# Sets of 4, 4, 4, 4 and 2 tiles, a third place for maxima, another order of first loads, and shifted urgencies in a planned order

## The chip, the core and the metric

The kernel runs on one core of a Trainium2 chip. The metric is the device time of one execution in microseconds (us), lower being better; the kernel before takes 776.19 us, the median of three runs (775.37 to 777.86).

## What is computed

Three layers follow one another on a batch of 4 sequences of 576 positions and 512 features.

```
scores = q k^T / 8, masked: 32 positions back (heads 0-3) or every 4th of 128 back (heads 4-7)
x   = softmax(scores) v                     # 4 x 8 heads x 576 x 64, joined to 4 x 576 x 512
h   = relu(x w_in)                          # 512 -> 1024
g   = sigmoid(conv3 over positions of h)
y   = (h * g) w_out                         # 1024 -> 512
u   = y + real(fft over features(fft over positions(y)))
un  = (u - mean(u)) / sqrt(var(u) + 1e-6)   # by row
out = u + relu(un w_ch1) w_ch2              # 512 -> 2048 -> 512
```

Rows of the output are held as 18 tiles of 128 positions by 512 features.

## The kernel before

**A planned order.** The program is first written down as a list of works (class `Plan`). A work is one instruction, or one group of matmuls that stay together (`products`), and it has the engines that may do it with a cost for each, its operands, and a `key`: the time by which it is wanted. `order()` lowers each key below those of the works that need it, and then simulates all engines with those costs; at each step the engine that is free first takes the work with the smallest key among those that are ready. The order that comes out is the order in which each engine's instructions are issued, and on the chip each engine works through its own in that order.

**Attention, stage one.** `tick(n)` does one of 56 pieces (14 for each of the 4 sequences; a piece is 4 blocks of queries of two heads). TensorE forms scores in PSUM (for sequences 0 and 1 a matmul with the mask goes first, and ScalarE copies the scores to a tile `sm`; for 2 and 3 VectorE adds the mask on the way to `sm`). GpSimd finds the maximum over partitions (`partition_all_reduce`, into a ring `mxs` of 2 tiles). VectorE subtracts it, ScalarE takes the exponential, TensorE multiplies with v (with a column of ones, for the sum). VectorE adds 1e-9 to the sums (tile `rs`) and takes the reciprocal; ScalarE scales the four blocks with it, in four instructions (`normed`, line 605, tile `xb`). TensorE transposes, ScalarE and VectorE write the result as a high and a low part (`copy`, `lo_of`) into `x`. Every product of stages two to four is made of three matmuls of such parts (`mm3`).

**The gated layer, stage two.** For each sequence and each of 8 blocks of 128 hidden features, `m1` makes two halves of 288 columns in PSUM, through one bank for the first three sequences, which ScalarE empties with a relu into `hp`; convolution, tanh and the gating follow on VectorE and ScalarE, and the result goes as high and low part to `hid_t`. `m2` uses four blocks of 128 columns of it as stationary operands, beginning at columns 0, 128, 288 and 416 (`COLS`), and adds into banks 4 to 7. The weights come as 64-bit floats in a staging tile `raw`, and VectorE turns each block into high and low part (`convert`: three bit operations, then a subtraction).

**The Fourier layer, stage three.** `dft(b)` takes a sequence's folded rows through tables (tile `tb`, loaded by GpSimd's DMA queue), adds to y and stores tiles of u. `ln` normalises rows: `bn_stats`, `bn_aggr` and 13 small VectorE operations for a group of tiles, then a ScalarE scaling, four transposes and a split for each tile. In `dft(1)` the tiles of the second set are normalised at once and stored (`to_dram`), among them tile 16, in a group of its own.

**The last layer, stage four.** The 18 tiles are worked through in sets (`SETS`: 4, 5, 5 and 4 tiles); for each set and each of 16 blocks of 128 hidden features, `n1` makes the hidden block for all tiles of the set and `n2` multiplies it, tile by tile, into one PSUM bank per tile. `n1` of a set of 4 is 12 matmuls of 512 columns. A set of 5 has 640 columns, more than a bank holds, so that `n1` is 24 matmuls of 320 columns. `n2` is three matmuls of 512 columns for each tile. `runs` gives the order of the sets and their banks; the first set begins inside stage three and is finished after the second. `lns` says in which steps of one set the next set's tiles are loaded and normalised.

Of the kernel before, what the change touches and what calls it, by code (L numbers as in the profile page):

```python
# [25 lines left out]
HS = S // 2  # L26
# [158 lines left out]

LAT = {"PE": 0.25, "DVE": 0.12, "ACT": 0.15, "POOL": 0.2, "SP": 0.0, "NO": 0.0}
# [5 lines left out]
class Plan:  # L192
# [98 lines left out]

    def order(self):
# [6 lines left out]
        for w in reversed(W):  # L299
            us = min(w.where.values()) + (2.0 if w.bytes else 0.0)  # L300
            for s in w.succ:
                w.key = min(w.key, W[s].key - us - 0.1)
# [115 lines left out]
def tile_kernel(ctx: ExitStack, tc: tile.TileContext, forms, qt_in, ktp, ktd, vtp, vtd, wm1, wm2, conv_w,  # L418
# [63 lines left out]
    hid_t = moe.tile([128, 2, 2, 640], F32R, "hid")  # L482
# [4 lines left out]
    gh_t, gl_t = ([hid_t[:, i, l, :S] for i in range(2)] for l in range(2))  # L487
# [54 lines left out]
    mxs = att.ring(2, [128, 384], F32, "mx")  # L542
    rss = att.ring(3, [128, 4], F32, "rs")
    xbs = att.ring(3, [128, 4, D], F32, "xb")
    tiny = att.tile([32, 8], F32, "tiny")

# [17 lines left out]
    def tick(n, sb, pb, at, spare_dve, less=False):  # L564
# [26 lines left out]
        with P.products(at + 5):  # L591
# [3 lines left out]
        dve("tensor_scalar", 0.15, out=rs.unsqueeze(2), in0=pv[:nq, :, 64:65], scalar1=1e-9, scalar2=None,  # L595
            op0=ALU.add)
# [9 lines left out]
        P.add({"ACT": 0.92} if less else {"DVE": 0.42}, normed, [pv[:nq, :, 0:64], rs], [xb])  # L606
# [34 lines left out]
    COLS = [0, 128, 288, 416]  # L641
    hid = {}

    def m1(b, f, h_banks, at):
# [24 lines left out]
        copy(gh, g, ("ACT", "POOL"))  # L669
        lo_of(gl, g, gh)  # L670

    def m2(b, f, at):
        gh, gl = hid[NF1 * b + f]
        w = W1.tiles[1, f]
        for i in range(4):
            c0 = COLS[i]
            with P.products(at + 2.15 * i):
                mm3(bank[4 + i], gh[:, c0:c0 + 128], gl[:, c0:c0 + 128], w[:, 0], w[:, 1], f == 0, f == NF1 - 1)
        for src, dst in ((gh, g9h), (gl, g9l)):
            sv = src.bitcast(F32).rearrange("p (t s) -> p t s", t=2)[:, :, 256:288]  # L680
# [161 lines left out]
    def dft(b, at, every):  # L842
# [94 lines left out]
        if bp:  # L937
            y9 = yload(16 + pr)
            finish(16 + pr, y9, *products(lambda l, c: t9[0][:, l, c], lambda l, c: t9[1][:, l, c], a09))
            if b == 1:  # L940
                ln([y9], [lambda: to_dram(8)], df, when[0] + 8)
# [5 lines left out]
    SETS = (range(0, 4), range(4, 9), range(9, 14), range(14, 18))  # L947
    R0 = 8
    runs = ((0, 0, R0, (4, 5, 6, 7)), (1, 0, 16, (0, 1, 4, 5, 6)), (0, R0, 16, (7, 0, 1, 4)),
            (2, 0, 16, (5, 6, 7, 0, 1)), (3, 0, 16, (4, 5, 6, 7)))  # L950
# [70 lines left out]
    dve("memset", 0.05, out=tiny)  # L1021
    P.run({"POOL": 7.0}, "partition_all_reduce", out_ap=tiny, in_ap=tiny, channels=32,
          reduce_op=bass_isa.ReduceOp.max, key=-100)
    P.key = -50
    P.key = -60
    for t in QT[:1]:
        dve("memset", 0.35, out=t[64:128, 0, :])
        dve("memset", 0.35, out=t[0:64, 1, :])
    dma(KT[0][:, 0:608], ktp[0])
# [198 lines left out]
```

## Time and profile before

| | before |
|---|---|
| median of 3 runs | 776.19 us (775.37 to 777.86) |
| the profiled execution | 778.47 us |
| its span, first to last instruction | 776.7 us |
| TensorE (PE) busy | 744.8 us (96%) |
| weight loads (PEld) busy | 663.2 us (85%) |
| VectorE (DVE) busy | 486.7 us (63%) |
| ScalarE (ACT) busy | 308.6 us (40%) |
| GpSimd (POOL) busy | 135.9 us (17%) |
| mean granted TensorE clock | 0.984 |

The span is part of the profiled execution's own time; 1.8 us lie around it. That execution was 2.3 us longer than the median of the runs. Matmuls are pipelined, so the time that a group of them takes is read from its start to the start of the next group, not from the durations. L259, L246 and L605 are lines of helpers through which many instructions pass, so that the names of the tiles tell what an instruction is.

### The profile page before, as it was taken

Reading aid. Unit: us, or ns where it says so; the run is one execution under the profiler, and the core shown is the slowest. Engines: PE = TensorE matmul, PEld = TensorE weight load, DVE = VectorE, ACT = ScalarE, POOL = GpSimd, SP = SyncE. Lnnn points to the kernel's source line nnn. Section 1 sums busy time; section 2 is a strip of 40 time slices with the busy share of each in tenths; the row PEclk is TensorE's granted clock in tenths of the full one; section 3 lists DMA queues with packets and bytes.
Section 4 is the critical chain, followed back from the end, with each engine's and each line's share of the span. In section 5 each row is a group of like instructions: output and inputs, shape, how many; then the busy total and the mean of one; then the engine's idle time right before and its main releaser. Section 6 shows DMA issues by size and latency. Waiting matters only on the chain.

```text
span 776.7 us, 11954 instructions
## 1 busy us (share of the span) xinstructions
PE 744.8 (96%) x4438; PEld 663.2 (85%) x4438; DVE 486.7 (63%) x1155; ACT 308.6 (40%) x792; POOL 135.9 (17%) x151
## 2 busy tenths in 40 slices
PE   5889989999999999989999999999999999999997
PEld 4779879998999998867788999988889999988886
DVE  5989989889888788979677667317544111121112
ACT  3877766675667655434332122112212111101110
POOL 4654424542445112201000000000000000000000
PEclk9979999999999999989999999999999999999999
DMA  9944354223412835357947333005131000030001
GB/s 239 254 152 134 107 164 139 88 72 111 152 48 90 285 120 163 107 190 250 330 162 246 136 133 135 1 1 163 42 105 32 28 1 1 1 122 1 1 0 55
DMA packets 38976, 88.58 MB, mean 114 GB/s; under 512 B 4351, under 2 KB 9859, under 8 KB 38790
## 3 DMA queue, kind: packets, MB, share of 16 engines
q1 hardware_dynamic: 38262, 84.66, 34.1%
q0 software_dynamic: 432, 2.97, 1.0%
q8 instruction: 35, 0.57, 0.3%
q10 hardware_dynamic: 224, 0.18, 0.1%
q14 instruction: 23, 0.19, 0.1%
HBM read 65.23 MB, written 22.44 MB: 113 GB/s over the span
## 4 chain that ended last, share of the span: by engine, by line
PE 53%; DVE 1%; ACT 0%; issue 0%; ACTq 0%
PE pb L259 53%; DVE y L246 0%; DVE hid L246 0%; DVE win L246 0%; DVE pm L246 0%; DVE raw L246 0%; DVE hp L246 0%; DVE pp L246 0%; ACT pq L246 0%; ACT pm L246 0%; ACTq L246 0%
## 5 line engine op out<-in xcount | busy, mean ns | idle before, releaser
L259 PE MATMUL pb<-wf,hid 128*128 128x512 f32 x1140 | 291.5, 397 | 1.2 <-DVE hid L246 1.2
L259 PEld LDWEIGHTS pb<-wf,hid 128*128 128x128 f32 x1140 | 207.6, 189 | 39.1 <-DVE hid L246 1.6
L246 DVE SCALAR_TENSOR_TENSOR hid<-pb,hid 128x320 fp32r<-128x320 f32 (+1 forms) x96 | 53.5, 557 | 186.5 <-ACT hid L246 186.4
L246 ACT ACTIVATE hid<-pb 128x320 fp32r<-128x320 f32 (+1 forms) x96 | 47.1, 491 | 256.7 <-PE pb L259 256.7
L259 PE MATMUL pb<-x,wf 128*128 128x288 f32 x768 | 116.6, 302 | 3.3 <-DVE wf L246 2.0
L259 PEld LDWEIGHTS pb<-x,wf 128*128 128x128 f32 x768 | 108.8, 191 | 7.0 <-DVE wf L246 2.2
L259 PE MATMUL pb<-unt,wf 128*128 128x320 f32 x672 | 103.6, 309 | 0.0
L259 PEld LDWEIGHTS pb<-unt,wf 128*128 128x128 f32 x672 | 100.8, 188 | 2.3
L246 POOL PARTITION_ALL_REDUCE mx<-sm x56 | 82.9, 1486 | 80.6 <-DVE sm L246 39.5
L259 PE MATMUL pb<-wf,wf 128*128 128x512 f32 x336 | 85.1, 400 | 3.6 <-DVE hid L246 3.6
L259 PEld LDWEIGHTS pb<-wf,wf 128*128 128x128 f32 x336 | 64.0, 193 | 17.5 <-DVE hid L246 4.3
L605 ACT ACTIVATE xb<-pb,rs 72x64 f32<-72x64 f32 (+1 forms) x224 | 51.2, 309 | 13.2 <-DVE rs L246 12.9
L246 DVE SCALAR_TENSOR_TENSOR cv<-hp,convw,cv 128x576 f32<-128x576 f32 x64 | 55.4, 866 | 1.3 <-ACT cv L246 0.7
L259 PEld LDWEIGHTS pb<-VT,sm 104*72 104x72 f32 (+1 forms) x448 | 41.0, 157 | 8.6 <-ACT sm L246 6.8
L259 PE MATMUL pb<-VT,sm 104*72 104x65 f32 (+1 forms) x448 | 42.8, 240 | 5.6 <-ACT sm L246 5.6
L259 PE MATMUL pb<-QT,KT 128*104 128x144 f32 (+1 forms) x224 | 44.3, 323 | 1.6 <-ACT sm L246 1.1
L259 PEld LDWEIGHTS pb<-QT,KT 128*104 128x104 f32 (+1 forms) x224 | 36.1, 191 | 7.5 <-issue 4.9
L246 ACT ACTIVATE hp<-pb 128x288 f32<-128x288 f32 x64 | 26.6, 416 | 29.9 <-PE pb L259 28.5
L246 DVE TENSOR_TENSOR wf<-raw,wf 128x512 fp32r<-128x512 f32 x44 | 31.7, 722 | 6.9 <-ACT wf L246 6.6
L246 DVE SCALAR_TENSOR_TENSOR raw<-raw,win 128x512 uint32<-128x512 uint32 x48 | 34.9, 727 | 0.9
L246 DVE SCALAR_TENSOR_TENSOR win<-raw,win 128x512 int32<-128x512 int32 x48 | 34.7, 723 | 1.0
L246 POOL CAST g<-hid 128x64 fp32r<-128x64 f32 x43 | 22.4, 528 | 73.4 <-ACT hid L246 37.1
(143 smaller groups left out, 842.6 us busy)
## 6 DMA issues: line engine op xcount, KB each, us to landing
raw<-in_wm_dram SPq DMA_DIRECT2D x48, 512.0 KB, 4.5
y<-yd SPq DMA_DIRECT2D x18, 256.0 KB, 4.2
ud<-y SPq DMA_DIRECT2D x18, 256.0 KB, 3.5
QT<-in_qt_dram SPq DMA_DIRECT2D x31, 144.0 KB, 3.4
fd<-fs SPq DMA_DIRECT2D x8, 514.0 KB, 3.9
fl<-fd SPq DMA_DIRECT2D x8, 514.0 KB, 6.3
yd<-y SPq DMA_DIRECT2D x16, 256.0 KB, 2.2
uu<-ud SPq DMA_DIRECT2D x16, 256.0 KB, 3.1
```

Source lines behind the costliest of these rows:

```text
L246: getattr(self.engines[eng], name)(**a)
L259: getattr(self.engines["PE"], name)(*[v.real() for v in a], **kw)
L605: nc.scalar.mul(out=x[:, i], in_=p[:, i], mul=r[:, i:i + 1])
```

## The change

It has seven parts. (1) `SETS` becomes 4, 4, 4, 4 and 2 tiles, with banks for each run, and `lns` follows. Tile 16 moves from the second set to the third, and so it is no longer normalised in `dft(1)`, but in stage four, with the other tiles of the third set. (2) `hid_t` grows from 640 to 768 columns, and stage two lays its two halves of 288 at columns 0 and 384, so that `m2` takes blocks beginning at 0, 128, 384 and 512. (3) The addition of 1e-9 to the sums goes from VectorE to ScalarE. (4) The scaling of `xb` goes to VectorE, as one instruction, for every second piece of the first 14; it stays on ScalarE otherwise. (5) `mxs` has three tiles. (6) The first loads are issued in another order: the bf16 identity and the first 384 columns of the mask by ScalarE's queue, k and q of the first unit (a unit is two heads of one sequence), then more of the mask, k and q of the second unit, v of the first, the other identity, k and q of the third, v of the second, and only then the first weight block `raw`; the memsets of `QT` get earlier keys. (7) After keys are lowered, 31 seeds each pick a stretch of keys (4 to 50 us long) and shift every key in it at random by up to 1, 2, 4 or 8 us; then keys are lowered again. The scratch for GpSimd's DMA descriptors goes from 2048 to 512 bytes.

```diff
--- before.py
+++ after.py
...
     __slots__ = ("where", "fn", "deps", "key", "bytes", "after", "start", "eng", "left", "ready", "succ", "id")
 
+
+NUDGES = (9, 12, 27, 33, 49, 53, 82, 92, 98, 130, 181, 284, 297, 353, 473,
+          503, 521, 594, 836, 1456, 1870, 2106, 2119, 2189, 2250, 2504, 2667, 2792, 3014, 3080,
+          3211,)
+
 LAT = {"PE": 0.25, "DVE": 0.12, "ACT": 0.15, "POOL": 0.2, "SP": 0.0, "NO": 0.0}
 
...
         return self.add({queue: 1.0 if queue == "POOL" else 0.42 if v.form.shape[0] == 128 else 0.58}, fn, ins, outs, key, nb)
 
+    def urgency(self):
+        W = self.works
+        for w in reversed(W):
+            us = min(w.where.values()) + (2.0 if w.bytes else 0.0)
+            for s in w.succ:
+                w.key = min(w.key, W[s].key - us - 0.1)
+
     def order(self):
         W = self.works
         for w in W:
...
         for w in W:
             for d in w.deps:
                 W[d].succ.append(w.id)
-        for w in reversed(W):
-            us = min(w.where.values()) + (2.0 if w.bytes else 0.0)
-            for s in w.succ:
-                w.key = min(w.key, W[s].key - us - 0.1)
+        self.urgency()
+        for seed in NUDGES:
+            rng = random.Random(seed)
+            a = rng.uniform(0, 560)
+            z = a + rng.uniform(4, 50)
+            amp = rng.choice((1, 2, 4, 8))
+            for w in W:
+                if a < w.key < z:
+                    w.key += rng.uniform(-amp, amp)
+        self.urgency()
         free = dict.fromkeys(("PE", "DVE", "ACT", "POOL", "SP", "NO"), 0.0)
         can = {e: {} for e in free}
         bus, drift = 0.0, 0.0
...
     win = stg.tile([128, 512], I32, "win")
     moe = pool_of("moe", reuse_waits="tile")
     x_odd = moe.tile([128, 4, 2, S], F32R, "x")
-    hid_t = moe.tile([128, 2, 2, 640], F32R, "hid")
+    hid_t = moe.tile([128, 2, 2, 768], F32R, "hid")
     cv_t = moe.tile([128, S], F32, "cv")
     g_t = moe.tile([128, S], F32, "g")
     hpad = [moe.tile([128, S + 2], F32, "hp") for _ in range(2)]
     moe.fill(-moe.size)
-    gh_t, gl_t = ([hid_t[:, i, l, :S] for i in range(2)] for l in range(2))
+
+    gh_t, gl_t = ([hid_t[:, i, l].rearrange("p (t s) -> p t s", t=2)[:, :, :HS] for i in range(2)] for l in range(2))
 
     low = pool_of("low", reuse_waits="tile")
     g9h, g9l = (low.tile([128, NF1, 128], F32R, "g9") for _ in range(2))
...
     QT = [att.tile([128, 2, S], F32, "QT") for _ in range(NS)]
     VT = [att.tile([128, 8, 2, 65], F32, "VT") for _ in range(NS)]
     sms = att.ring(5, [128, 384], F32, "sm")
-    mxs = att.ring(2, [128, 384], F32, "mx")
+    mxs = att.ring(3, [128, 384], F32, "mx")
     rss = att.ring(3, [128, 4], F32, "rs")
     xbs = att.ring(3, [128, 4, D], F32, "xb")
     tiny = att.tile([32, 8], F32, "tiny")
+    eps = att.tile([128, 1], F32, "eps")
 
     def kq_load(u):
         b, hp = divmod(u, 4)
...
     xT = {b: x_even if b % 2 == 0 else x_odd for b in range(B)}
     subs = [(u, t) for u in range(16) for t in range(3 if u % 4 < 2 else 4)]
 
-    def tick(n, sb, pb, at, spare_dve, less=False):
+    def tick(n, sb, pb, at, spare_dve):
 
         u, t = subs[n]
         b, hp = divmod(u, 4)
...
             for s in range(4):
                 mm(pv[:nq, s, :], sm[:, s * nq:(s + 1) * nq], vt[:nk, 2 * t + s // 2, s % 2, :], True, True)
         rs, xb = rss()[:nq], xbs()[:nq]
-        dve("tensor_scalar", 0.15, out=rs.unsqueeze(2), in0=pv[:nq, :, 64:65], scalar1=1e-9, scalar2=None,
-            op0=ALU.add)
+        P.run({"ACT": 0.21}, "activation", out=rs.unsqueeze(2), in_=pv[:nq, :, 64:65], func=AF.Identity,
+              bias=eps[:nq], scale=1.0)
         dve("reciprocal", 0.17, out=rs, in_=rs)
 
         def normed(eng):
...
             else:
                 for i in range(4):
                     nc.scalar.mul(out=x[:, i], in_=p[:, i], mul=r[:, i:i + 1])
-        P.add({"ACT": 0.92} if less else {"DVE": 0.42}, normed, [pv[:nq, :, 0:64], rs], [xb])
+        P.add({"DVE": 0.42} if n < 14 and n % 2 else {"ACT": 0.92}, normed, [pv[:nq, :, 0:64], rs], [xb])
         bt = pb[:, 260:260 + 2 * nq]
         with P.products(at + 8):
             for i in range(2):
...
         dve("tensor_tensor", 0.1, out=convw, in0=a, in1=r, op=ALU.add)
 
-    COLS = [0, 128, 288, 416]
+    COLS = [(0, 0), (0, 128), (1, 0), (1, 128)]
     hid = {}
 
     def m1(b, f, h_banks, at):
...
         dve("scalar_tensor_tensor", 0.48, out=g[:, 289:576], in0=cv[:, 575:288:-1], scalar=1.0,
             in1=hp[:, 576:289:-1], op0=ALU.add, op1=ALU.mult)
         gh, gl = hid[s] = gh_t[s % 2], gl_t[s % 2]
-        copy(gh, g, ("ACT", "POOL"))
-        lo_of(gl, g, gh)
+        gs = g.rearrange("p (t s) -> p t s", t=2)
+        copy(gh, gs, ("ACT", "POOL"))
+        lo_of(gl, gs, gh)
 
     def m2(b, f, at):
         gh, gl = hid[NF1 * b + f]
         w = W1.tiles[1, f]
         for i in range(4):
-            c0 = COLS[i]
+            t, c0 = COLS[i]
             with P.products(at + 2.15 * i):
-                mm3(bank[4 + i], gh[:, c0:c0 + 128], gl[:, c0:c0 + 128], w[:, 0], w[:, 1], f == 0, f == NF1 - 1)
+                mm3(bank[4 + i], gh[:, t, c0:c0 + 128], gl[:, t, c0:c0 + 128], w[:, 0], w[:, 1], f == 0, f == NF1 - 1)
         for src, dst in ((gh, g9h), (gl, g9l)):
-            sv = src.bitcast(F32).rearrange("p (t s) -> p t s", t=2)[:, :, 256:288]
+            sv = src.bitcast(F32)[:, :, 256:288]
             dv = dst[:, f, :].rearrange("p (t s) -> p t s", t=2)[:, :, 32 * (b % 2):32 * (b % 2) + 32]
             P.run({"ACT": 0.235, "POOL": 0.45}, "copy", out=dv, in_=sv)
 
...
         if bp:
             y9 = yload(16 + pr)
             finish(16 + pr, y9, *products(lambda l, c: t9[0][:, l, c], lambda l, c: t9[1][:, l, c], a09))
-            if b == 1:
-                ln([y9], [lambda: to_dram(8)], df, when[0] + 8)
         pair(0)
 
 
-    SETS = (range(0, 4), range(4, 9), range(9, 14), range(14, 18))
+    SETS = (range(0, 4), range(4, 8), range(8, 12), range(12, 16), range(16, 18))
     R0 = 8
-    runs = ((0, 0, R0, (4, 5, 6, 7)), (1, 0, 16, (0, 1, 4, 5, 6)), (0, R0, 16, (7, 0, 1, 4)),
-            (2, 0, 16, (5, 6, 7, 0, 1)), (3, 0, 16, (4, 5, 6, 7)))
+    runs = ((0, 0, R0, (4, 5, 6, 7)), (1, 0, 16, (0, 1, 4, 5)), (0, R0, 16, (6, 7, 0, 1)),
+            (2, 0, 16, (4, 5, 6, 7)), (3, 0, 16, (0, 1, 4, 5)), (4, 0, 16, (6, 7)))
     hidden, rings, sets = {}, {}, []
 
     def un_load(p):
...
 
     dve("memset", 0.05, out=tiny)
+    P.add({"DVE": 0.05}, lambda _: nc.vector.memset(eps.real(), 1e-9), [], [eps], -95)
     P.run({"POOL": 7.0}, "partition_all_reduce", out_ap=tiny, in_ap=tiny, channels=32,
           reduce_op=bass_isa.ReduceOp.max, key=-100)
-    P.key = -50
-    P.key = -60
-    for t in QT[:1]:
+
+    for i, t in enumerate(QT):
+        P.key = -80 + i
         dve("memset", 0.35, out=t[64:128, 0, :])
         dve("memset", 0.35, out=t[0:64, 1, :])
-    dma(KT[0][:, 0:608], ktp[0])
+    loads = [-90.0]
+
+    def first(out, in_, queue="SP"):
+        loads[0] += 1
+        dma(out, in_, key=loads[0], queue=queue)
+
+    first(ident16, ident16_in, "ACT")
+    first(maskt[:, :384], mask[:, :384], "ACT")
+    first(KT[0][:, 0:608], ktp[0])
     for h, queue in ((0, "SP"), (1, "ACT")):
-        dma(QT[0][64 * h:64 * h + 64, h, :], qt_in[0, 64 * h:64 * h + 64], queue=queue)
-    dma(ident16, ident16_in, queue="ACT")
-    dma(maskt[:, :768], mask[:, :768])
-    P.key = -50
-    for t in QT[1:]:
-        dve("memset", 0.35, out=t[64:128, 0, :])
-        dve("memset", 0.35, out=t[0:64, 1, :])
+        first(QT[0][64 * h:64 * h + 64, h, :], qt_in[0, 64 * h:64 * h + 64], queue)
+    first(maskt[:, 384:768], mask[:, 384:768])
+    P.key = loads[0] + 1
+    kq_load(1)
+    P.key += 1
+    v_load(0)
+    P.key += 1
+    dma(ident, ident_in)
+    P.key += 1
+    kq_load(2)
+    P.key += 1
+    v_load(1)
+    P.key += 1
     dma(raws[0], wm1[0, :, 0])
-    v_load(0)
-    dma(ident, ident_in)
-    P.key = -40
-    kq_load(1)
-    v_load(1)
-    P.key = -30
-    kq_load(2)
+    P.key += 1
     dma(maskt[:, 768:], mask[:, 768:])
     v_load(2)
+    P.key += 1
     dma(raws[1], wm1[1, :, 0])
     P.key = 1e9
     for t in hpad:
...
         _, i, f = W1.todo[k]
         W1.convert(place[i, f], raws[k % 2], k > 1)
 
-    EARLY, LESS = 16, 56
+    EARLY = 16
     LEAD = 8.0
 
     def ticks(b):
...
             else:
                 sb, pb = bank[0], of("v2", [1, 3])
             at = 1.6 * n if b == 0 else T0 + PER * (b - 1) - LEAD + m * (PER - 3.0) / 14
-            tick(n, sb, pb, at, b < 2, n < LESS)
+            tick(n, sb, pb, at, b < 2)
 
     def mlp1(b, f0, f1, h_banks):
         step = PER / NF1
...
             step = 1.38 * len(SETS[runs[r][0]])
             begin[r, f] = at, step
             at += step
-    lns = ({(2, 9 + i): (2, (i,)) for i in range(5)})
+    lns = {(2, 9 + i): (2, (i,)) for i in range(4)}
     lns.update({(3, 3 + i): (3, (i,)) for i in range(4)})
+    lns.update({(4, 5 + i): (4, (i,)) for i in range(2)})
     for k, (r, f) in enumerate(seq):
         if (r, f) == (1, 0):
             later = pool_of("set", "left", (low,), reuse_waits="tile")
-            sets.append(later.tile([128, 2, 4, 640], F32R, "unt"))
+            sets.append(later.tile([128, 2, 4, 512], F32R, "unt"))
             un_load(1)
         if (r, f) == (1, 2):
             wpb = pool_of("wpb", "right", (D_["pool"], keep), reuse_waits="tile")
...
 
     sketch = _bacc.Bacc("TRN2", target_bir_lowering=False, num_devices=1)
     forms = tile.TileContext(sketch).__enter__().alloc_tile_pool(name="forms", bufs=1)
-    nc = _bacc.Bacc("TRN2", target_bir_lowering=False, num_devices=1, dynamic_dma_scratch_size=2048)
+    nc = _bacc.Bacc("TRN2", target_bir_lowering=False, num_devices=1, dynamic_dma_scratch_size=512)
     arrays, args = {}, []
     for name, a in _layout(**inputs).items():
         arrays[f"in_{name}_dram"] = a
```

## Rows read from the trace of the kernel before

**Rows 1.** Stretches (us): each engine's busy time, instructions, granted clock, DMA share, GB/s.
```profile
0.00:47.40 47.40, 30.93 (x230) 27.44 (x231) 36.23 (x94) 30.36 (x104) 25.37 (x24) 0.90 0.93 243
90.00:118.00 28.00, 24.09 (x162) 21.67 (x162) 25.02 (x51) 17.34 (x46) 7.37 (x7) 0.94 0.38 121
118.00:300.00 182.00, 182.00 (x1270) 167.57 (x1269) 160.63 (x370) 119.93 (x325) 68.23 (x75) 1.00 0.39 128
...
334.00:346.00 12.00, 8.39 (x28) 6.33 (x28) 8.93 (x27) 3.06 (x7) 1.41 (x2) 0.72 0.44 158
346.00:385.00 39.00, 36.52 (x204) 30.68 (x202) 31.64 (x83) 16.93 (x38) 2.39 (x5) 1.00 0.85 284
385.00:770.00 385.00, 385.00 (x2023) 338.35 (x2024) 150.86 (x366) 73.59 (x145) 2.34 (x4) 1.00 0.21 69
```

**Rows 2.** Waits of the whole span: engine and tile, waited for; us, times, longest.
```profile
ACT hp L246 <- PE pb L259: 28.5, 37, 2.7
...
DVE rs L246 <- PE pb L259: 8.8, 13, 2.8
```

**Rows 3.** TensorE's timeline: start, us, operation, count; steps and groups of matmuls.
```profile
283.47 4.34 PE L259 MATMUL pb<-wf,hid 128*128 128x512 f32 x18
287.64 3.35 PE L259 MATMUL pb<-x,wf 128*128 128x288 f32 x24
...
401.27 1.61 PE L259 MATMUL pb<-tb,t 128*128 128x258 f32 x12
...
402.72 0.28 PE L259 MATMUL pb<-tb,a 128*128 128x258 f32 x1
...
418.87 3.68 PE L259 MATMUL pb<-unt,wf 128*128 128x320 f32 x24
...
425.81 3.68 PE L259 MATMUL pb<-unt,wf 128*128 128x320 f32 x24
...
707.20 2.88 PE L259 MATMUL pb<-x,hid 128*128 128x512 f32 x12
...
712.63 2.88 PE L259 MATMUL pb<-x,hid 128*128 128x512 f32 x12
```

**Rows 4.** Instructions by line and shape, stage four's hidden block: busy us, mean ns.
```profile
L246 DVE SCALAR_TENSOR_TENSOR hid<-pb,hid 128x320 fp32r<-128x320 f32 x64 | 31.4, 491 | 109.2 <-ACT hid L246 109.2
...
L246 ACT ACTIVATE hid<-pb 128x320 fp32r<-128x320 f32 x64 | 28.0, 438 | 145.6 <-PE pb L259 145.6
```

**Rows 5.** Timeline of VectorE and TensorE about tile 16's normalisation.
```profile
335.78 0.69 DVE L246 BATCH_NORM_STATS2 st<-y 128x6 f32<-128x512 f32 x1
...
338.91 0.16 DVE L246 SCALAR_TENSOR_TENSOR sq<-mv,sq 128x1 f32<-128x1 f32 x1
...
340.10 5.43 PE L259 MATMUL pb<-wf,wf 128*128 128x512 f32 x12 [3.61 <-DVE hid L246]
```

**Rows 6.** Timeline of the head: first matmul, first weight block, first m1.
```profile
7.41 0.48 PE L259 MATMUL pb<-maskt,ident 128*128 128x384 bf16 x1 [7.41 <-DMA maskt<-in_mask_dram]
...
9.36 0.43 DVE L246 TENSOR_SCALAR win<-raw 128x512 int32<-128x512 int32 x1 [3.13 <-DMA raw<-in_wm_dram]
...
47.44 3.33 PE L259 MATMUL pb<-x,wf 128*128 128x288 f32 x12
```

**Rows 7.** Tile rs (ns min/median/max), then instructions by line and shape (mean ns).
```profile
L605 ACT ACTIVATE xb<-pb,rs x224: 290/309/354, 15.4 to 250.4; 72x64 f32<-72x64 f32 x64, 96x64 f32<-96x64 f32 x48
L246 DVE TENSOR_SCALAR rs<-pb x56: 144/151/163, 15.0 to 249.3; 72x4 f32<-72x4 f32 x32, 96x4 f32<-96x4 f32 x24
...
L246 ACT CAST a<-a 1x32 fp32r<-1x32 f32 x8 | 1.5, 215 | 0.4 <-DVE a L246 0.3
```

**Rows 8.** DMA issues (us to landing), then timeline: the tables' issue and first use.
```profile
tb<-in_tab_dram POOLq DMA_DIRECT2D x1, 1161.0 KB, 14.6
...
250.28 1.76 POOL L288 DMA_DIRECT2D tb<-in_tab_dram  x3
...
266.57 0.96 PE L259 MATMUL pb<-tb,fl 128*1 128x290 f32 x6
```

More of the change, by code (lines that the diff above doesn't have):

```diff
@@ L1 @@
+import random
 from contextlib import ExitStack, contextmanager
```

## The prediction

> **What bounds the kernel now.** I read the stretches first [rows 1]. From 385 to 770 us TensorE is busy for the whole time at the full clock, and so it is from 118 to 300: there whatever shortens TensorE's own work shortens the kernel, and relief of other engines does nothing. The rest is lost elsewhere. From 0 to 47.4 TensorE is idle for 16.5 us, and a granted clock of 0.90 means that it ran at the lower of its two levels (1.2 instead of 2.4 GHz) for 9.5 us, half of which is lost work. From 90 to 118 it idles 3.9 us, with 1.7 more lost to a clock of 0.94 (3.4 us at the lower level). From 334 to 346 it idles 3.6 us, and a clock of 0.72, which is 6.7 us at the lower level, loses 3.4 more. From 346 to 385 it idles 2.5 us. VectorE is busy for 25.0 of 28 us in the second of these places and 31.6 of 39 in the last, so it is what TensorE waits for. Then I read the waits [rows 2] and the timelines [rows 3, 5, 6] for the prices.
>
> **Sets of 4, 4, 4, 4, 2.** A step of a set of 5 takes 425.81 - 418.87 = 6.94 us for 39 matmuls with 15,360 columns, a step of a set of 4 takes 712.63 - 707.20 = 5.43 us for 24 matmuls with 12,288 columns [rows 3]. The two give 16.9 ns for each matmul and 0.409 ns for each column: 6.94 - 1.25 x 5.43 = 0.15 us is left for 39 - 1.25 x 24 = 9 matmuls. The columns of stage four stay the same in sum. The matmuls of n1 fall from 32 x 24 + 32 x 12 = 1152 to 80 x 12 = 960, and 192 x 16.9 ns = 3.2 us. A step of the new set of two is then 18 x 16.9 ns + 6144 x 0.409 ns = 2.82 us, a shape that the trace does not have. Its nearest row is a group of 12 matmuls of 258 columns, 402.72 - 401.27 = 1.45 us [rows 3], against the 1.46 us that the two figures give for 12 of 256, so I keep the 3.2. The ends: a matmul of 256 columns costs at least its columns (105 ns) and at most one of 320 columns (148 ns), against 121.6; over 192 matmuls that is 3.2 us better or 5.1 worse, so the part is worth -1.9 to 6.4. What must stay hidden in the short step is the hidden block: ScalarE and VectorE take 0.44 + 0.49 us at 320 columns [rows 4], less at 256, while n1 of the next block covers 1.45. Half a microsecond is left for the handovers; each 0.1 us beyond it would cost 16 x 0.1 = 1.6 us.
>
> The Trainium skill (page "TensorE: Matmul & The Clock Gate", section "Back-to-back issue gap") gives the spacing of warm matmuls as columns / 2.4 GHz plus 2.5 ns. By that rule 192 matmuls fewer would save 0.5 us instead of 3.2. The steps above show a fixed part of 16.9 ns; the measurement decides.
>
> **Tile 16 out of stage three.** Its normalisation holds VectorE from 335.78 to 339.07 us, 3.3 us in fifteen small operations [rows 5]. Behind it on VectorE, which works in order, stands the low part of a hidden block, and TensorE waits 3.61 us for that. Then 12 matmuls of 512 columns last 5.43 us [rows 5], where 12 such last 2.88 at the full clock [rows 3]. Idle time and clock together cost this stretch 3.6 + 3.4 = 7.0 us. With the normalisation gone the block is ready 3.3 us earlier. So the part is worth at most 7.0, and nothing if other work takes the place. What is late next is the conversion of weight blocks, also on VectorE, busy 31.6 of the 39 us that follow. I take 5.5. In stage four the same operations are hidden: VectorE is busy 151 of 385 us there [rows 1]. The tile's four transposes cost TensorE the same in either place.
>
> **Halves at 0 and 384.** A group of 18 matmuls of m2 takes 287.64 - 283.47 = 4.17 us [rows 3], while 18 matmuls of 512 columns by the figures above would take 4.07. Half of them take their weights from columns 288 and 416. If the beginning column is the cause, these cost 11 ns more each, and the kernel has 4 x 8 x 2 x 3 = 192 of them: 2.1 us. If it is not, nothing. One group does not separate the two; I take 1.5. The copies into the gapped halves move the same elements, and I cost them at nothing: TensorE is the bound from 118 to 300.
>
> **Attention's ends.** The addition leaves VectorE 56 times, 56 x 0.151 = 8.5 us [rows 7], and comes to ScalarE 56 times. The trace has no such instruction; the nearest is a ScalarE cast of 1 x 32 at 0.215 us [rows 7], so about 12 us. For seven pieces of the first 14 the four scalings (4 x 0.309 us [rows 7]) become one VectorE operation on 256 columns, which the trace does not show either; 0.49 us for 320 columns [rows 4] bounds it above. So within the first 14 pieces ScalarE loses 8.7 - 3.0 = 5.7 us of work, and VectorE gains at most 3.4 - 2.1 = 1.3. In the head the two have 30.4 and 36.2 us of work in 47.4 [rows 1], and a piece goes through both by turns, so m1, which begins at 47.44 [rows 6], can come earlier by 0 to 5.7 us. I take 2.5, a little under half, since nothing but the chain of pieces holds m1 there and its other half is VectorE's. After the head the addition stands in ScalarE's line 42 more times. I cost it at nothing as long as ScalarE is early: it waited 28.5 us for TensorE before its relus [rows 2]. The price without that cover is in the rivals. The third place for maxima is worth nothing by itself: GpSimd is busy 25.4 of 47.4 us.
>
> **First loads.** The first matmul starts at 7.41 us, when the mask has landed [rows 6]. Half of the mask now goes first. The scores need k and q too, so I take 1.0 us (0 to 2). Against it, the first weight block, whose conversion VectorE begins at 9.36 us after 3.13 idle [rows 6], moves on SP's queue behind k and q of two units and v of two, and it is wanted in stage two, where VectorE is nearly full until 118. It costs 0 to 3.1, at most that idle time again. I take 0.5.
>
> **Shifted keys and the scratch.** The shifts reorder everything up to some 560 us of planned time. Their price has no row. They can clear at most what is idle or slow from 90 to 118 and idle from 346 to 385, 5.6 + 2.5 = 8.1 us, or add a stall like that at 334, 7.0 us. Nothing in the trace says which, so I take 0. The smaller scratch matters to the three loads of the tables: issued from 250.28, landed 14.6 us later at most, first used at 266.57 [rows 8]. Some 2 us are spare. I take 0.
>
> **The sum.** 3.2 + 5.5 + 1.5 + 2.5 + 1.0 - 0.5 = 13.2 us. The profiled execution took 778.47 us (span 776.7 and 1.8 around it), which gives 765.3. It was 2.3 us longer than the median of the runs, so the forecast for the median is 776.2 - 13.2 = 763 us.
>
> **Rivals.**
>
> A. The stall moves on. Another chain of VectorE's work, the weight conversions, stands where the normalisation stood, and what the head gains is waited for again between 90 and 118. For it: VectorE's share in both places. Against it: the 3.3 us leave VectorE for good. What is left is TensorE's own work, 3.2 + 1.5 = 4.7: 771.5 us.
>
> B. The new order also clears the 8 us of the other two places: 755 us. For it: VectorE loses 8.5 us of additions spread over the first 250 us. Against it: its work before 118 hardly shrinks.
>
> C. Matmuls cost by their columns alone, and the sets are worth nothing. Against it: the 0.15 us of a step [rows 3]. Time: 763 + 3.2 = 766. This is what the page's small fixed part would nearly make of it.
>
> D. The other side: ScalarE's line. From 47.4 to 250 us the addition waits, in order, for its product with v, and behind it stand the relus that empty the one bank of m1. VectorE waited 8.8 us at the additions in all, 0.16 for each of 56 [rows 2]. If each of the 42 later pieces holds TensorE for that and for the 0.22 us of the operation, 0.38 x 42 = 16 us are lost: 776.2 - 13.2 + 16 = 779. It decides from 13.2 / 42 = 0.31 us for each piece. Against it: ScalarE is busy 120 of 182 us from 118 to 300 and waits for TensorE, not the reverse.
>
> **How the numbers follow.** I give the forecast 0.49, A 0.20, B 0.18, C 0.07, D 0.06. The forecast's own range is 759 to 768 (the stall worth 2.5 to 7, the head 1 to 5). The range of 8 in 10 reaches below nearly to B's time, since B may come in part, and above past A's: 753 to 773. Only D and the worst of A lie above it. Within 0.3% is 773.9 to 778.5, about what a measurement of this kernel can tell from no change. Faster: the forecast, B, C and most of A, 0.88. Same: the rest of A, where the parts cancel, 0.06. Slower: D, 0.06.
>
> **What would show it.** Steps of sets of 4 at 5.43 us throughout and of the last set at 2.8. A chain of waits made of TensorE alone from about 370 us on. No gap of 3.6 us before the hidden blocks near 330, and a clock of 1.00 there. Groups of 18 matmuls of m2 at 4.07 us. m1 beginning near 44 us, and the first matmul near 6.4. Wrong it would be if TensorE's idle time from 90 to 385 us stayed near the 10 us of [rows 1] in new places, if steps of the last set were over 3.0 us, or if TensorE waited for relus of ScalarE.

## The result and the profile after

The changed kernel takes 757.65 us (median of 4 runs, 757.01 to 761.7) against 776.46 for the kernel before: a ratio of 0.9773, interval 0.9753 to 0.9792, or 18.8 us less. The forecast was 763 and the range 753 to 773. The profiled execution took 757.01 us, with a span of 755.2. TensorE is busy for 736.6 us of it (744.8 before) and idle for 18.6 (31.9 before).

The stretches of the changed kernel, in the columns of [rows 1]:

```profile
0.00:47.40 47.40, 37.78 (x283) 34.55 (x284) 36.94 (x93) 31.49 (x108) 30.47 (x27) 0.93 0.86 233
47.40:90.00 42.60, 41.21 (x305) 37.22 (x304) 41.14 (x77) 33.30 (x101) 21.55 (x21) 1.00 0.47 144
90.00:118.00 28.00, 26.56 (x189) 24.09 (x188) 26.69 (x55) 21.08 (x59) 9.93 (x10) 1.00 0.48 157
118.00:300.00 182.00, 181.76 (x1266) 166.85 (x1265) 160.11 (x348) 119.96 (x334) 73.94 (x88) 1.00 0.38 123
300.00:334.00 34.00, 34.00 (x198) 29.96 (x197) 30.70 (x85) 17.19 (x40) 3.23 (x7) 1.00 0.66 229
334.00:346.00 12.00, 10.16 (x59) 7.98 (x59) 11.70 (x29) 6.30 (x13) 2.90 (x4) 1.00 0.57 209
346.00:385.00 39.00, 39.00 (x236) 34.14 (x235) 31.09 (x70) 14.38 (x38) 1.08 (x3) 1.00 0.73 246
385.00:748.00 363.00, 363.00 (x1709) 304.00 (x1708) 138.15 (x333) 65.75 (x113) 1.63 (x2) 1.00 0.20 64
```

After 47.4 us the granted clock is 1.00 everywhere, where 90 to 118 had 0.94 and 334 to 346 had 0.72. A second execution of the same kernel (760.49 us, the last run below) shows the same clock there, but 22.6 us of idle time, so that a difference of some us in idle time between two single executions proves little. Idle time is left in the head (9.6 us, 16.5 before), a little up to 118, and 1.8 us near 340. VectorE is busy 11.70 of 12 us there, so it is still what TensorE waits for, but only briefly. The end of the chain of waits (start, us, engine and line):

```profile
343.70 0.46 DVE a L253
344.16 0.04 issue
344.20 406.98 PE pb L266 x1967
```

TensorE runs without a gap from 344.20 us to the end of its work (from 384.95 in the kernel before). What the kernel gained beyond shorter steps was therefore gained before 344.

TensorE's timeline, as in [rows 3] and [rows 6]: first matmul, first m1, groups of m2, the stretch of the old stall, steps of a set of 4 and of the set of 2.

```profile
5.12 0.48 PE L266 MATMUL pb<-maskt,ident 128*128 128x384 bf16 x1 [5.12 <-DMA maskt<-in_mask_dram]
...
41.32 2.66 PE L266 MATMUL pb<-x,wf 128*128 128x288 f32 x12
...
329.07 4.24 PE L266 MATMUL pb<-wf,hid 128*128 128x512 f32 x18
333.15 2.88 PE L266 MATMUL pb<-wf,wf 128*128 128x512 f32 x12
335.87 1.04 PE L266 MATMUL pb<-ident,y 128*128 128x128 f32 x8
336.66 2.99 PE L266 MATMUL pb<-wf,wf 128*128 128x512 f32 x12
340.85 0.96 PE L266 MATMUL pb<-tb,fl 128*1 128x290 f32 x6 [1.20 <-DVE ns L253]
...
404.45 2.88 PE L266 MATMUL pb<-unt,wf 128*128 128x512 f32 x12
407.17 2.88 PE L266 MATMUL pb<-wf,hid 128*128 128x512 f32 x12
409.89 2.43 PE L266 MATMUL pb<-unt,wf 128*128 128x512 f32 x10
...
712.99 1.60 PE L266 MATMUL pb<-unt,wf 128*128 128x256 f32 x12
714.42 1.55 PE L266 MATMUL pb<-wf,hid 128*128 128x512 f32 x6
715.80 1.60 PE L266 MATMUL pb<-unt,x 128*128 128x256 f32 x12
```

A step of 4 tiles takes 409.89 - 404.45 = 5.44 us, a step of 2 takes 715.80 - 712.99 = 2.81 (forecast 2.82). The 18 matmuls of m2 take 333.15 - 329.07 = 4.08 us (4.17 before, forecast 4.07). The normalisation of tile 16 and its 3.61 us of idle time are gone.

The operations that the trace of before did not have, by line and shape (busy us, mean ns, idle before):

```profile
L253 ACT ACTIVATE rs<-pb,eps 72x4 f32<-72x4 f32 x32 | 8.2, 256 | 5.6 <-PE pb L266 4.9
...
L253 DVE SCALAR_TENSOR_TENSOR hid<-pb,hid 128x256 fp32r<-128x256 f32 x16 | 6.8, 425 | 36.7 <-ACT hid L253 36.7
...
L253 ACT ACTIVATE rs<-pb,eps 96x4 f32<-96x4 f32 x24 | 6.1, 262 | 5.1 <-PE pb L266 4.8
L253 ACT ACTIVATE hid<-pb 128x256 fp32r<-128x256 f32 x16 | 6.1, 383 | 41.5 <-PE pb L266 39.0 <-DVE hp L253 2.4
...
L624 DVE TENSOR_TENSOR xb<-pb,rs 96x256 f32<-96x256 f32 x3 | 1.3, 421 | 0.2
```

ScalarE's additions take 14.3 us in all (estimate: 12) and the scaling on VectorE 0.42 us. In the short step the hidden block takes 0.38 + 0.43 us and stays hidden: no matmul there waits.

### The profile page after: what moved, and what is told of

It is laid out like the page before. It is cut to its first block, busy times and chain, and to the rows that moved or that the text cites. A ratio compares the mean times of both kernels' runs of the same rounds, so it can differ in the third digit from the quotient of the medians.

```text
span 755.2 us, 11432 instructions
## 1 busy us (share of the span) xinstructions
PE 736.6 (98%) x4246; PEld 641.1 (85%) x4246; DVE 478.3 (63%) x1087; ACT 309.8 (41%) x800; POOL 144.7 (19%) x159
## 4 chain that ended last, share of the span: by engine, by line
PE 54%; DVE 1%; issue 0%
PE pb L266 54%; DVE fo L253 0%; DVE ns L253 0%; DVE fs L253 0%; DVE hp L253 0%; DVE o L253 0%; DVE f L253 0%; DVE a L253 0%
## 5 line engine op out<-in xcount | busy, mean ns | idle before, releaser
L253 DVE SCALAR_TENSOR_TENSOR hid<-pb,hid 128x512 fp32r<-128x512 f32 (+1 forms) x80 | 51.0, 637 | 183.3 <-ACT hid L253 183.2
L253 ACT ACTIVATE hid<-pb 128x512 fp32r<-128x512 f32 (+1 forms) x80 | 44.5, 556 | 248.2 <-PE pb L266 231.8
L266 PEld LDWEIGHTS pb<-x,wf 128*128 128x128 f32 x768 | 106.9, 189 | 3.0 <-ACT hp L253 0.7
L266 PE MATMUL pb<-unt,wf 128*128 128x512 f32 (+1 forms) x504 | 103.5, 354 | 0.0
L253 POOL PARTITION_ALL_REDUCE mx<-sm x56 | 88.3, 1591 | 62.5 <-ACT sm L253 26.8
L266 PEld LDWEIGHTS pb<-unt,wf 128*128 128x128 f32 x504 | 85.0, 189 | 14.2
L266 PE MATMUL pb<-wf,wf 128*128 128x512 f32 x336 | 82.0, 391 | 0.0
L627 ACT ACTIVATE xb<-pb,rs 72x64 f32<-72x64 f32 (+1 forms) x196 | 44.4, 306 | 4.8 <-DVE rs L253 4.7
L253 DVE TENSOR_TENSOR sm<-sm,mx 104x288 f32<-104x288 f32 (+1 forms) x56 | 32.1, 574 | 8.5 <-POOL mx L253 8.2
L253 POOL CAST g<-hid 128x64 fp32r<-128x64 f32 x48 | 25.1, 532 | 53.4 <-ACT hid L253 28.9
```

The costliest lines, as they stand in the source:

```text
L253: getattr(self.engines[eng], name)(**a)
L266: getattr(self.engines["PE"], name)(*[v.real() for v in a], **kw)
L627: nc.scalar.mul(out=x[:, i], in_=p[:, i], mul=r[:, i:i + 1])
```

## Experiments

Each kernel was timed beside the kernel before on the same chip (775.5 to 775.6 us). A difference in us is (ratio - 1) x 775.5. The texts speak of the **planned end**: the time at which, by the plan's own costs, the last work ends when `order()` simulates the engines. It is a figure of the program, not a measurement.

### Which part gave what

**The shifts taken out** of the changed kernel.

```diff
-NUDGES = (9, 12, 27, 33, 49, ...
+NUDGES = ()
```

> The changed kernel with the list of seeds empty, so that no key is shifted; all else as in the change. Theory P (the parts add up, and the shifts clear only what is left of the idle places before 385 us): 2 to 6 us above the changed kernel's 757.7, so 760 to 764, with TensorE's idle time up by as much between 0 and 400 us and stage four unchanged. Theory S (the gain beyond the sets and the halves is made by the shifts): 10 us or more above it, 768 or later, with a stall of VectorE's making near 335 us again.

767.38 us, ratio 0.9901 (0.988 to 0.9922). All parts but the shifts give 7.7 us together, and the shifts 9.7, between the two theories' ranges; the stall near 335 us that theory S expected does not come back. TensorE's waits in this kernel from 90 to 120 and from 300 to 385, out of its timeline, and the end of its chain of waits:

```profile
93.55 0.70 PE L264 MATMUL pb<-VT,sm 104*72 104x65 f32 x8 [0.71 <-DVE x L251]
...
95.92 1.58 PE L264 MATMUL pb<-x,wf 128*128 128x288 f32 x10 [0.70 <-DVE wf L251]
...
106.21 1.72 PE L264 MATMUL pb<-x,wf 128*128 128x288 f32 x10 [2.34 <-DVE wf L251]
...
302.97 1.36 PE L264 MATMUL pb<-ident,y 128*128 128x128 f32 x8 [1.84 <-ACT y L251]
...
346.44 0.66 PE L264 MATMUL pb<-ident,y 128*128 128x128 f32 x4 [1.39 <-ACT y L251]
...
353.70 1.07 PE L264 MATMUL pb<-tb,fl 128*128 128x290 f32 x6 [0.65 <-DVE a L251]
...
353.70 406.91 PE pb L264 x1967
```

The stall of tile 16 is gone here too. What is left is above all a weight block converted too late at 106 (`wf`) and two waits for `y`. In the changed kernel neither stands; the short wait for `a` does (0.64 us at 344.20). In this pair of profiles TensorE's idle time falls from 24.6 to 18.6 us, and its busy time from 740.1 to 736.6 for the same 4246 matmuls; in this trace 90 to 118 has a clock of 0.94. In the second execution of the changed kernel the idle time is 22.6 us and the busy time 736.1, so the shorter busy time is seen in both and the idle time is not as sure.

**Sets and tile 16 alone**, put into the kernel before.

```diff
-            if b == 1:
-                ln([y9], [lambda: to_dram(8)], df, when[0] + 8)
...
-    SETS = (range(0, 4), range(4, 9), range(9, 14), range(14, 18))
+    SETS = (range(0, 4), range(4, 8), range(8, 12), range(12, 16), range(16, 18))
```

> The kernel before with the sets of 4, 4, 4, 4 and 2 tiles alone, and with them tile 16's normalisation moved from stage three to stage four; no shifts. By the steps of the prediction 3.2 us from stage four and up to 7 from the stall near 335 us: 766 to 770 beside 775.6 to 776.5 for the kernel before. Rival: only the 3.2 us of stage four come, and a stall appears elsewhere between 300 and 385 us: 772 to 773. Theory Q (the time follows the end that order() itself works out while it plans): that end is 761.7 us for this list and 768.7 for the kernel before, so 7 us less.

766.71 us, ratio 0.988 (0.9846 to 0.9914): 9.3 us faster. With 3.2 for the steps, 6 are left for tile 16 (an inference: the two were not separated). TensorE waits 2.4 us from 300 to 385 in this kernel, against 7.1 in the kernel before.

**The normalisation of tile 16 put back** into the changed kernel, as work whose result nothing reads; the tile is still normalised in stage four. Once with the seeds and once without any.

```diff
+            if b == 1:
+                ln([y9], [lambda: to_dram(8)], df, when[0] + 8)
```

> The changed kernel with the normalisation of tile 16 left in stage three as well (its result is stored and not used; stage four normalises the tile again as in the change). VectorE has 3.3 us more to do near 335 us. Theory P: the time rises by 3 to 7 us, 761 to 765, with TensorE waiting for VectorE between 320 and 350 us. Rival: the planned order with its shifts finds room for it, and the rise is under 1 us.

> The changed kernel without shifts and with tile 16's normalisation left in stage three as well (its result is stored and not used). Beside the one without shifts (767.4) it has 3.3 us more for VectorE near 335 us and no other draw of the shifts, which the earlier run with both had. If the normalisation costs what stood at 336 us before: 3 to 7 us more, 770 to 774. If the 21 us of the earlier run were its doing: 780 or more. Theory Q: the plan's own end rises from 761.5 to 763.3, so 2 us more.

With the seeds 779.2 us, ratio 1.0062 (1.0041 to 1.0083): 21.5 us over the changed kernel, which no theory had. Without, 770.61, ratio 0.9941 (0.9921 to 0.996): 3.1 us over the kernel without shifts. In each stretch of keys that holds one of the added works, every later random draw falls on another work, so the first of these kernels has shifts of other works; it says nothing of the normalisation and much of the seeds. The second shows the mechanism. Its VectorE and TensorE timelines:

```profile
331.80 0.69 DVE L251 BATCH_NORM_STATS2 st<-y 128x6 f32<-128x512 f32 x1
...
334.93 0.16 DVE L251 SCALAR_TENSOR_TENSOR sq<-mv,sq 128x1 f32<-128x1 f32 x1
...
335.37 0.68 DVE L251 SCALAR_TENSOR_TENSOR hid<-pb,hid 128x512 fp32r<-128x512 f32 x1
```

```profile
336.11 4.61 PE L264 MATMUL pb<-wf,wf 128*128 128x512 f32 x12 [3.58 <-DVE hid L251]
340.56 0.60 PE L264 MATMUL pb<-ident,y 128*128 128x128 f32 x4
```

The fifteen small operations take the same 3.3 us, the low part of the hidden block stands behind them, TensorE waits 3.58 us (3.61 in [rows 5]), and the 12 matmuls after it take 4.45 us instead of 2.7, at a clock of 0.86 from 334 to 346. These lose 5 us; in their place the kernel without shifts waits 3.2 us for `y`, and the net is 3.1.

**Halves at 288.** Only the addresses change; the order of the instructions stays.

```diff
-    gh_t, gl_t = ([hid_t[:, i, l].rearrange("p (t s) -> p t s", t=2)[:, :, :HS] ...
+    gh_t, gl_t = ([hid_t[:, i, l, :S].rearrange("p (t s) -> p t s", t=2) ...
```

> The changed kernel with the halves of the hidden block at columns 0 and 288 again; the order of all instructions is the same as in the changed kernel, only addresses differ. If the beginning column is what costs: m2 groups of 18 take 4.17 us instead of 4.08, and the whole 1.9 us more than the changed kernel, about 759.5. If it is not: m2 groups unchanged and a time within 0.5 us of the changed kernel.

757.94 us, ratio 0.9777 (0.9763 to 0.9792), which the changed kernel's 757.65 can't be told from. Its trace is finer. The same 18 matmuls, and its first m1 and the end of its chain:

```profile
41.63 2.83 PE L266 MATMUL pb<-x,wf 128*128 128x288 f32 x12
...
330.20 4.29 PE L266 MATMUL pb<-wf,hid 128*128 128x512 f32 x18
334.33 2.89 PE L266 MATMUL pb<-wf,wf 128*128 128x512 f32 x12
...
345.30 406.98 PE pb L266 x1967
```

They take 4.13 us against 4.08, and 9 of the 18 have moved, so that each costs some 5.6 ns more; a group of 21 takes 4.84 against 4.78 us, one of 12 takes 2.87 against 2.83. So in these groups the beginning column does cost; 192 x 5.6 ns would be 1.1 us in the kernel. That estimate is too high. TensorE's unbroken run begins 1.1 us later, at 345.30 instead of 344.20, but 0.3 of it is there at the first m1 and 0.7 at 115 us. Matched matmul by matmul (the order is the same), this trace falls 0.37 us behind that of the changed kernel from 118 to 344 us, 0.40 of it at the 312 matmuls `wf,hid`, where the second execution of the changed kernel falls 0.04 behind the first. Nearly half of these 312 have moved, so the mean cost is under 3 ns each, and some 0.5 us in the kernel (an estimate from 0.40 us).

**Attention's ends alone**, in the kernel before.

```diff
-        dve("tensor_scalar", 0.15, out=rs.unsqueeze(2), in0=pv[:nq, :, 64:65], scalar1=1e-9, ...
+        P.run({"ACT": 0.21}, "activation", out=rs.unsqueeze(2), in_=pv[:nq, :, 64:65], ...
...
-        P.add({"ACT": 0.92} if less else {"DVE": 0.42}, normed, ...
+        P.add({"DVE": 0.42} if n < 14 and n % 2 else {"ACT": 0.92}, normed, ...
```

> The kernel before with attention's ends alone: the addition of 1e-9 on ScalarE, and every second scaling of the first 14 on VectorE. By the prediction m1 starts 2.5 us earlier (0 to 5.7) and the time falls by as much, to 771 to 775. Rival (the head's gain is waited for again between 90 and 118 us, where VectorE is full): m1 earlier, the time unchanged at 775 to 777. Rival D (ScalarE's line holds up the relus): 779 or more. Theory Q: the plan's own end falls from 768.7 to 765.8, so 3 us less.

774.19 us, ratio 0.9982 (0.996 to 1.0004): 1.4 us faster, which can't be told from nothing. Its first m1 begins at 46.59 instead of 47.44.

**The order of first loads alone**, in the kernel before: the lines of the change from `for i, t in enumerate(QT)` to the second `raw`.

```diff
-    dma(KT[0][:, 0:608], ktp[0])
...
+    first(ident16, ident16_in, "ACT")
+    first(maskt[:, :384], mask[:, :384], "ACT")
+    first(KT[0][:, 0:608], ktp[0])
```

> The kernel before with the new order of the first loads alone. By the prediction the first matmul comes 1 to 2 us earlier and the first weight block's conversion later, with 0.5 us left of it: 774 to 776. Rival: the late weight block costs its 3 us between 90 and 118, 777 to 779. Theory Q: the plan's own end rises from 768.7 to 770.3, so 1.6 us more.

779.26 us, ratio 1.0048 (1.0028 to 1.0067): 3.7 us slower. Its trace has a first m1 at 43.80, 3.6 us earlier, and then this (stretches):

```profile
0.00:47.40 47.40, 34.91 (x257) 31.15 (x258) 36.72 (x97) 31.01 (x111) 29.24 (x27) 0.89 0.87 232
47.40:90.00 42.60, 38.75 (x286) 35.80 (x286) 36.84 (x81) 29.71 (x89) 25.37 (x21) 0.97 0.41 127
```

The kernel before, in the second of these stretches:

```profile
47.40:90.00 42.60, 42.17 (x312) 39.74 (x311) 39.48 (x84) 31.29 (x95) 21.12 (x21) 0.95 0.40 129
```

What the head gained, 4.0 us of TensorE's busy time, the next stretch gave back all but 0.6 of: 38.75 us busy against 42.17. The late weight block is not what this trace shows as the price: from 40 to 120 us TensorE waits 2.8 us for weight blocks, and 2.9 in the kernel before. The profiled execution (776.54) was the fastest of ten, and its unbroken run begins earlier than that of the kernel before (383.08 against 384.95), so where the 3.7 of the median lie it does not show.

### Shifts, or these seeds?

**Other seeds**, 31 in a row, not picked.

```diff
-NUDGES = (9, 12, 27, 33, 49, ...
+NUDGES = (100001, 100002, ..., 100031)
```

> The changed kernel with 31 other seeds (100001 to 100031), which nobody picked. Theory P: about what the kernel without shifts takes, give or take 4 us, 757 to 767, since a shift of a key matters little. Theory S, that the seeds were picked for their effect: later than the kernel without shifts, 766 or more, as random shifts of 31 stretches make stalls as often as they remove them.

766.59 us, ratio 0.9881 (0.9852 to 0.9911), like no seeds at all (767.38). These unpicked shifts are worth nothing that can be told from noise.

**The change's seeds in the kernel before**, by `urgency()` and the loop over `NUDGES` alone.

> The kernel before with the 31 seeds as the only change. Its planned end goes from 768.7 to 777.5 us. Theory Q (the seeds fit the one list of works for which they were picked, and elsewhere they are noise): slower than before by 1 to 9 us, 777 to 785. Rival (shifted keys help whatever the list, by some 5 to 10 us): 766 to 771.

777.7 us, ratio 1.0026 (1.0009 to 1.0043): 2.0 us slower. The seeds that help the changed kernel's list of works do not help this one.

**Another list, with and without seeds of its own.** The changed kernel with the first loads in the order of before: without seeds, and with 37 seeds picked by the planned end.

```diff
-    first(ident16, ident16_in, "ACT")
-    first(maskt[:, :384], mask[:, :384], "ACT")
...
+    dma(KT[0][:, 0:608], ktp[0])
...
+    dma(raws[0], wm1[0, :, 0])
```

> The changed kernel without any seeds and with the first loads in the order of the kernel before. Its planned end is 761.8 us, against 761.5 for the changed kernel without seeds, which took 767.4. Theory Q (the time follows the planned end): 767 to 768. Rival F (the new order of loads costs 3.7 us by itself, as it did when put alone into the kernel before, since the first weight block comes late): 763 to 764.

> The changed kernel, but the first loads in the order of the kernel before, and 37 other seeds, picked one after the other because each brought the planned end of the last work forward: it is 751.4 us instead of 754.6 with the change's own loads and seeds. Theory Q (the time follows the planned end, plus 3 to 9 us that the costs of the plan miss): 754 to 758 us, at or below the changed kernel's 757.7. Theory F (what the plan does not see at the head, the wait for the first weight block, is what the old order of loads also avoids on the chip): below 755 us. Rival R (the change's seeds were picked on the chip and fit it; seeds picked by the plan alone lose part of the 9.7 us): 759 to 764 us.

> The changed kernel as it is, beside the others on the same chip: 757 to 758 us.

Without seeds 769.65 us, ratio 0.9919 (0.9897 to 0.9942). With its own 37, 759.02, ratio 0.978 (0.9761 to 0.9799). The changed kernel beside them: 758.74, ratio 0.9779 (0.9759 to 0.9799). So a search over seeds gives this list 10.8 us too, and the two kernels end level; the 3 us that its planned end was ahead did not come. Nor did the loss that rival R expected of seeds picked by the plan alone. The old order of loads, without seeds, is 1.4 us slower than the new one (0.9919 against 0.9901, the intervals overlapping): the 3.7 us that the new order costs in the kernel before are not found among the other parts, and the 763 to 764 of rival F did not come.

Planned end and time stand side by side in this table, each as a difference to the kernel before, in us:

| kernel | planned end | time |
|---|---|---|
| the change | -14.0 | -17.1 to -17.6 |
| without shifts | -7.2 | -7.7 |
| other seeds | -4.8 | -9.2 |
| tile 16 also, with the seeds | +4.7 | +4.8 |
| tile 16 also, no seeds | -5.3 | -4.6 |
| sets and tile 16 alone | -6.9 | -9.3 |
| attention's ends alone | -2.9 | -1.4 |
| first loads alone | +1.6 | +3.7 |
| the seeds alone | +8.9 | +2.0 |
| old loads, no seeds | -6.9 | -6.3 |
| old loads, 37 seeds | -17.2 | -17.1 |

The sign is the same in all eleven (the -1.4 of attention's ends can't be told from 0), and the difference is up to 7 us. Seeds 0, 1, 2 and so on, each kept only if it brings the planned end of the changed kernel forward, give the first 19 of the change's 31; its next 12 are others than the change's, so how those were found is not known. With the 37 seeds that were picked by that end and gave 10.8 us, and the 31 unpicked ones that gave nothing, this shows what the shifts are: a search over orders by that end.

## Why the prediction was right, and where its sum was not

The direction and the range held, and the time lies between the forecast's own range (759 to 768) and rival B's 755. Of the 18.8 us the forecast had 13.2, and the parts that made these 13.2 gave 7.7. That the time came out so near is in part luck: the parts with a price fell 5.5 us short, the shifts, put at 0, gave 9.7, and the two errors lie on opposite sides. Without the shifts TensorE still idles 7.9 us from 90 to 385, near the 10 that the prediction named as a sign of being wrong; with them it is 3.5.

- **Sets of 4, 4, 4, 4, 2**: 3.2 us forecast. The steps are 5.44 and 2.81 us (2.72 by columns alone), so the fixed 16.9 ns for a matmul hold at 256 columns too, and rival C falls. By the isolated warm spacing in the Trainium skill (page "TensorE: Matmul & The Clock Gate", section "Back-to-back issue gap") 18 matmuls with 6144 columns would take 2.6 us, an estimate; the step measured is 2.81, and the measurement decides.
- **Tile 16 out of stage three**: 5.5 forecast, 6 with the sets in the kernel before, 3.1 when undone in the kernel without shifts. The step is right, and so is its cause: with the normalisation put back, the stall of 3.58 us stands there again. What it is worth depends on what is late next, and this is rival A in part: the kernel without shifts takes 767.4, half-way from the forecast's 763 to rival A's 771.5, with waits for `y` (3.2 us) and for `wf` (4.1 in the whole span).
- **Halves at 0 and 384**: 1.5 forecast, some 0.5 by the traces matched matmul by matmul, at most 1.1; the whole time doesn't resolve it.
- **Attention's ends**: 2.5 forecast, 1.4 (-0.3 to 3.1) measured. The earlier m1 that it was to come from is small alone (46.59 against 47.44) and absent without shifts and with the old loads (47.96). Rival D falls: the ends alone are not slower, and in the changed kernel ScalarE waited 9.8 us for TensorE at the additions, and TensorE 0.5 us for a relu.
- **First loads**: +0.5 net forecast, -3.7 alone in the kernel before, +1.4 among the other parts, which is within noise. The first matmul starts at 5.12 us (forecast 6.4), and the first m1 at 41.32 (43.87 in the second execution; forecast 44; by itself this part brings it 3.6 us forward), but alone 3.4 of the 4.0 us of busy time were given back before 90 us. The forecast named the late weight block as the price and bounded it by 3.1; the trace shows no longer waits for weight blocks, and what costs the 3.7 stays open. Taking an earlier start for a gain of as much was not sound.
- **Shifted keys and the scratch**: 0 forecast with bounds of -7.0 and +8.1; the shifts gave 9.7. This is the step of the sum that failed. I counted only the idle time that the trace of before has from 90 to 118 and 346 to 385, and held the sign open. But the shifts act on what the other parts leave, the waits near 303, 346 and 106. By these traces the head is not among the places: the first m1 begins at 41.32 and 43.87 in two executions of the changed kernel and at 42.14 without shifts, and from there to the unbroken run it is 302.9 and 303.8 us against 311.6. And the shifts have a sign, since `order()` simulates the order and seeds can be picked by its end. I had that function before me and treated its input as noise. Rival B named the size and the places; its reason, that VectorE loses its additions, is not what cleared them, since the kernel without shifts has lost them too.
- **The scratch**: 0 forecast, not run alone. The tables were not late: issued from 239.06, landed 11.8 us later at most and first used at 258.82.

The parts as measured do not add. The sum 3.2 + 6 + 0.5 + 1.4 - 3.7 = 7.4 us comes near the 7.7 for all but the shifts, but only because the loads stand in it at -3.7, which they do not cost among the other parts. The kernel without shifts and with the old loads is the test: 3.2 + 6 + 0.5 + 1.4 = 11.1 us by its parts, 6.3 measured, and the sets and tile 16 alone gave 9.3. With intervals of 2 us or so on each, some 5 us are lost where the parts meet, or to the two parts that were not run alone; which, stays open.

What stays open: the third place for maxima and the scratch were not run alone, and why the time keeps up to 7 us apart from the planned end was not looked into. The 37 seeds with the old loads are as fast as the change and not faster, so no version beats it.

## What to carry to other kernels

Work out a part's price from steps of the trace, but ask of every removed stall what is late next: here the parts without the shifts fell 5.5 us short of 13.2. Random shifts of a planner's priorities are not noise if someone could pick the seeds by the planner's own end; then they are a search, worth 10 us here with two different lists, each with seeds of its own, and a loss in the two other lists that were given the change's seeds (2.0 us in the kernel before, 8.6 with the normalisation put back, 779.2 against 770.61). Measure a part beside the kernel without seeds, or the seeds hide it.

## What was not expected of the hardware

Two executions of the changed kernel differ by 3.5 us before TensorE's unbroken run (344.20 and 347.69), and 2.6 of them come at one place. The first execution:

```profile
33.51 0.42 DVE L253 TENSOR_SCALAR win<-raw 128x512 int32<-128x512 int32 x1
...
34.85 0.42 DVE L253 TENSOR_TENSOR sm<-sm,mx 104x288 f32<-104x288 f32 x1
34.88 3.08 POOL L253 PARTITION_ALL_REDUCE mx<-sm  x2 [1.41 <-DVE win L253]
...
35.75 0.32 PE L266 MATMUL pb<-ident,xb 72*128 72x72 f32 x2 [0.90 <-DVE rs L253]
```

The second:

```profile
34.96 3.31 POOL L253 PARTITION_ALL_REDUCE mx<-sm  x2 [1.41 <-ACT sm L253]
...
35.07 1.00 DVE L253 TENSOR_SCALAR win<-raw 128x512 int32<-128x512 int32 x1 [1.39 <-DMA raw<-in_wm_dram]
...
36.99 0.99 DVE L253 TENSOR_TENSOR sm<-sm,mx 104x288 f32<-104x288 f32 x1
...
38.46 0.47 PE L266 MATMUL pb<-ident,xb 72*128 72x72 f32 x2 [3.52 <-ACT sm L253]
```

The weight block landed later (the five loads of `raw` took 8.5 us in the middle instead of 5.9), its conversion stands in VectorE's line ahead of the attention's subtraction, and TensorE waited 3.52 us instead of 0.90. The late load is only part of it: VectorE began the conversion 1.56 us later, and then the conversion's first operation and the subtraction lasted 1.00 and 0.99 us instead of 0.42 each, 1.15 us more, while GpSimd's reductions ran. In this execution the 13 subtractions of this shape that no operation of GpSimd overlaps took 0.46 us at most, and the 19 others up to 0.99. By these rows it is the late load together with the work of GpSimd into which it moved VectorE's; which operations of the two engines disturb each other was not tested. `order()` counts with fixed costs and foresees neither.
